# Regrouping the selection chains and moving evictions in a Fourier and mixture-of-experts kernel

## The chip, the cores and the metric

The kernel runs on one core of a Trainium2 chip. The metric is the time of one execution on the device, in microseconds (us); lower is better. A time is the median of several runs. The profile is of one further execution, with its own time. Engines are named as in the profile: PE is TensorE's matmul, PEld its weight load, DVE is VectorE, ACT is ScalarE, POOL is GpSimd and SP is SyncE, whose queue issues most of the transfers.

## The reference

For each of 8 batches of 3136 rows by 256 columns, a spectral layer runs first: a real Fourier transform along the rows, a complex 256x256 product with bias, a soft threshold of 0.01, and the inverse transform. Then comes a small routed network: each row gets a score, the 128 rows with the highest score in their batch go through a two-layer network, and the result is added to these rows.

```
X = rfft(x, axis=1)
Yr = Xr @ w_r - Xi @ w_i + b_r;  Yi = Xr @ w_i + Xi @ w_r + b_i
Y = soft_threshold(Yr) + 1j * soft_threshold(Yi)
x = irfft(Y, n=3136, axis=1)                      # the output, but for the routed rows
scores = einsum('bsd,d->bs', x, w_gate)
for b in range(8):
    top = argpartition(-scores[b], 128)[:128]
    h = maximum(x[b, top] @ w1, 0);  ye = h @ w2
    out[b, top] = x[b, top] + sigmoid(scores[b, top])[:, None] * ye
```

## The kernel before

**The stream.** The transform of length 3136 is split into 98 by 32. A loop over steps t (lines 588 to 616) writes out a software pipeline. A batch takes 13 steps of the middle stages and 16 items of the outer ones. In each step the loop issues, for the batch and item that it has reached: the first transform stage `s1` (16 steps ahead of the middle), the second stage `s2`, the product and threshold `spectral`, the first inverse stage `s2i`, and the last inverse stage `s1i` (17 steps behind). `s2i` of batch b is complete in program order at step 13b+13, and `s1i` of batch b at about 13b+29. `s1` works on batches 5 to 7 in steps 49 to 87 and is at its end there; `s2i` ends at step 104, and `s1i` at step 120.

Each item of `s1` is three matmuls into a PSUM tile `s` of 98x512, which is copied to SBUF tile `at`: items with an even number by ScalarE (line 406), items with an odd number by VectorE (line 404). Scratch tensors `As` and `Cs` in DRAM carry the data between the outer and the middle stages.

**The selection.** Scores come out of `s2i` with no further pass. `route` (lines 522 to 532) is a generator, a thread that the loop advances twice in each step. It waits until `s2i` is done with each batch of its group, runs `score` for it, then `select` for the whole group, then `place` for each batch in turn. `select` (lines 233 to 276) looks for the value of the 128th highest score bit by bit: with 2 bits per round it takes 17 rounds, with 3 bits per round 12. A round is a chain: VectorE makes candidate thresholds (`f`, line 247), compares the scores with them (`c`, line 250) and counts along rows (`n`, line 255); PE sums the counts over the partitions (`tot`, line 260); VectorE compares the totals (`ok`, `d`, lines 270 and 272) and updates the value (`w`, line 273). A group of more than one batch takes one round per step, a group of one batch two. The groups before are batches 0 to 2, batches 3 and 4 (2 bits each), and 5, 6 and 7 alone (3 bits each). The last thread, batch 7's, is issued at high priority. `place` (lines 278 to 324) turns the threshold into 128 row numbers, `idx`, one small tile for each batch.

**The routed network (FFN below).** `fetch` gathers a batch's selected rows from the output in DRAM (line 329, on POOL's queue) once its `s1i` is issued and its `idx` exists, with at most two batches fetched and not done. `ffn` takes the batches in order: four ticks of waiting, `prepare` (two transposes, line 337, and their copy to `xT`), `hidden` twice (16 matmuls each, line 354, then ScalarE makes `hh` and VectorE `hl`), `combine` (24 matmuls, line 366, then VectorE makes `ye` and POOL's queue scatters it, line 369). These two threads advance once in each step, so a batch takes eight steps. Their instructions on PE are kept behind the `s1i` matmul of the same step. Batches 0 to 3 use PSUM tile `m`, a single buffer that `score`, `select` and `place` use too; batches 4 to 7 use the tiles `px` and `py` of the middle stages. For the last batch but one, `combine` waits until the last batch is fetched, and the last batch's `prepare` is issued ahead of it. After the loop, the threads that are left are advanced until they end.

Counted in the code before: the chain of batches 0 to 2 has its rounds in steps 41 to 58, that of 3 and 4 in 67 to 84, batch 5's in 80 to 86, batch 6's in 93 to 99 and batch 7's in 106 to 112. `combine` falls in steps 67, 75, 83, 93, 101, 109 and 120 for batches 0 to 6; batch 7's FFN comes after the loop.

Of the kernel before, what the change touches and what calls it, by code (L numbers as in the profile page):

```python
# [12 lines left out]
BF16 = mybir.dt.bfloat16  # L13
U32 = mybir.dt.uint32
# [5 lines left out]
B, S, D = 8, 3136, 256  # L20
N1, N2 = 98, 32
# [87 lines left out]
def fourier_moe(ctx: ExitStack, tc: tile.TileContext, x, w_r, w_i, b_r, b_i, wg, w1, w2,  # L109
# [3 lines left out]
    NCHK = -(-cap // 128)  # L113
    const = ctx.enter_context(tc.tile_pool(name="const", bufs=1))
    pool = ctx.enter_context(tc.tile_pool(name="work", bufs=2))
# [10 lines left out]
    def c_tile(shape, dt, name):  # L126
        t = const.tile(shape, dt, name=name)
        size = int(np.prod(shape[1:])) * (2 if dt == BF16 else 4)
        placed[0] += -(-size // 32) * 32
        if placed[0] % 64:  # L130
            const.tile([128, 8], F32, name=name + "_pad")
            placed[0] += 32
        return t
# [23 lines left out]
    nrow = c_tile([N1, 1], F32, "nrow")  # L157
    tcol = c_tile([128, NCHK], F32, "tcol")
    scores = c_tile([N1, B, N2], F32, "scores")
    digits = c_tile([N1, 256], U32, "digits")  # L160

    def queued(eng, f):
# [70 lines left out]
    def select(bs, bits, thrs):  # L233
        nb = bs.stop - bs.start
        tag = f"_{bs.start}"
        sv = scores[:, bs, :].rearrange("p b (o c) -> p b o c", o=1)
        cuts = [31]
        while cuts[-1] > 0:
            cuts.append(max(cuts[-1] - bits, 0))
        w = None  # L240
        for hi, i in zip([32] + cuts, cuts):
            m = 2 ** (hi - i) - 1
            f = pool.tile([N1, nb, m], U32, name="f" + tag, bufs=1)
            if w is None:
                nc.vector.memset(f, 0)
            else:
                nc.vector.tensor_tensor(out=f, in0=digits[:, 8 * i:8 * i + m].rearrange("p (o m) -> p o m", o=1).broadcast_to([N1, nb, m]),
                                        in1=w.broadcast_to([N1, nb, m]), op=ALU.bitwise_xor)
            c = pool.tile([N1, nb, m, N2], BF16, name="c_5" if nb == 1 else "c" + tag, bufs=1)
            nc.vector.tensor_tensor(out=c, in0=sv.broadcast_to([N1, nb, m, N2]),  # L250
                                    in1=f.bitcast(F32).rearrange("p b (m o) -> p b m o", o=1).broadcast_to([N1, nb, m, N2]),
                                    op=ALU.is_ge)
            n = pool.tile([N1, nb, m], BF16, name="n" + tag, bufs=1)
            with nc.allow_low_precision(reason="counts up to 28 are exact"):
                nc.vector.tensor_reduce(out=n, in_=c, axis=AX.X, op=ALU.add)
            yield
            if nb > 1:
                yield
            tot = ps.tile([N1, nb, m], F32, name="m", bufs=1)
            nc.tensor.matmul(tot, ones, n, start=True, stop=True)  # L260
            w2 = pool.tile([N1, nb, 1], U32, name="w" + tag)
            if w is None:
                nc.vector.tensor_scalar(out=w2.bitcast(I32), in0=tot, scalar1=cap - 0.5, scalar2=1.0, op0=ALU.is_ge, op1=ALU.subtract)
            else:
                d = pool.tile([N1, nb, 1], U32, name="d" + tag, bufs=1)
                if m == 1:
                    nc.vector.tensor_scalar(out=d, in0=tot, scalar1=cap - 0.5, scalar2=None, op0=ALU.is_ge)
                else:
                    ok = pool.tile([N1, nb, m], F32, name="ok" + tag, bufs=1)
                    nc.vector.tensor_scalar(out=ok, in0=tot, scalar1=cap - 0.5, scalar2=None, op0=ALU.is_ge)  # L270
                    with nc.allow_low_precision(reason="whole numbers"):
                        nc.vector.tensor_reduce(out=d, in_=ok, axis=AX.X, op=ALU.add)
                nc.vector.scalar_tensor_tensor(out=w2, in0=d, scalar=i, in1=w, op0=ALU.logical_shift_left, op1=ALU.bitwise_xor)
            w = w2
        for b in range(bs.start, bs.stop):
            thrs[b] = w.bitcast(F32)[:, b - bs.start, :]

    def place(b, thr, slots):
        m = pool.tile([N1, 2, N2], BF16, name="mask")
        nc.vector.tensor_scalar(out=m[:, 0, :], in0=scores[:, b, :], scalar1=thr, scalar2=None, op0=ALU.is_gt)  # L280
        nc.vector.tensor_scalar(out=m[:, 1, :], in0=scores[:, b, :], scalar1=thr, scalar2=None, op0=ALU.is_equal)
        mf = m.rearrange("p a c -> p (a c)")
        yield
        pt = ps.tile([2 * N2, N1], F32, name="m", bufs=1)
        nc.tensor.matmul(pt, mf, eye, start=True, stop=True)
        mt = pool.tile([2 * N2, N1], BF16, name="mt")
        nc.vector.tensor_copy(mt, pt)
        yield
        pp = ps.tile([N1, 2, N2], F32, name="m", bufs=1)
        nc.tensor.matmul(pp.rearrange("p a c -> p (a c)"), mt, upper[:2 * N2, :], start=True, stop=True)  # L290
        row = pool.tile([N1, 2, N2 + 2], F32, name="row")
        nc.vector.tensor_copy(row[:, :, :N2], pp)
        cnt = pool.tile([N1, 2], BF16, name="cnt")
        nc.vector.tensor_copy(cnt, pp[:, :, N2 - 1])
        for a in range(2):
            nc.vector.tensor_copy(row[:, a, N2 + 1:], nrow)
        yield
        pb = ps.tile([N1, 2], F32, name="m", bufs=1)
        nc.tensor.matmul(pb, lower, cnt, start=True, stop=False)
        nc.tensor.matmul(pb[:, 1:2], ones, cnt[:, 0:1], start=False, stop=True)  # L300
        nc.vector.tensor_copy(row[:, :, N2], pb)
        end = pool.tile([N1, 2], F32, name="end")
        nc.vector.tensor_tensor(out=end, in0=row[:, :, N2], in1=row[:, :, N2 - 1], op=ALU.add)
        for k in range(NCHK):
            n = min(128, cap - 128 * k)
            hot = pool.tile([N1, 2, n], F32, name="hot", bufs=1)
            io = iota[:N1, 128 * k:128 * k + n]
            for a in range(2):
                nc.vector.tensor_scalar(out=hot[:, a, :], in0=io, scalar1=row[:, a, N2:N2 + 1], scalar2=None, op0=ALU.is_ge)
                nc.vector.scalar_tensor_tensor(out=hot[:, a, :], in0=io, scalar=end[:, a:a + 1], in1=hot[:, a, :],  # L310
                                               op0=ALU.is_lt, op1=ALU.mult)
            yield
            pi = ps.tile([n, N2 + 2], F32, name="m", bufs=1)
            for a in range(2):
                nc.tensor.matmul(pi, hot[:, a, :], row[:, a, :], start=(a == 0), stop=(a == 1))
            r = pool.tile([n, 1], F32, name="r")
            nc.vector.tensor_tensor(out=r, in0=tcol[:n, k:k + 1], in1=pi[:, N2:N2 + 1], op=ALU.subtract)
            le = pool.tile([n, N2], F32, name="le")
            c = pool.tile([n, 1], F32, name="col")
            nc.vector.tensor_scalar(out=le, in0=pi[:, :N2], scalar1=r, scalar2=None, op0=ALU.is_le)  # L320
            nc.vector.tensor_reduce(out=c, in_=le, axis=AX.X, op=ALU.add)
            idx = pool.tile([n, 1], U32, name=f"idx{b}_{k}", bufs=1)
            nc.vector.tensor_tensor(out=idx, in0=c, in1=pi[:, N2 + 1:], op=ALU.add)
            slots[b, k] = idx

# [66 lines left out]
    def s1(b, i):  # L392
        if i == 0:
            As[b] = dram.tile([N1, N2, D], F32, name="As")
        if i % 2 == 0:
            at[b] = pool.tile([N1, 4, D], F32, name="at", bufs=3)
        o = 2 * (i % 2)
        p = ps.tile([N1, 2, D], F32, name="s", bufs=4)
        if b == 0:
            nc.tensor.matmul(p, w1f, xt.pop((b, i))[:, o:o + 2, :], start=True, stop=True)  # L400
        else:
            mm3(p, w1h, w1l, *xs.pop((b, i)))
        if i % 2:
            nc.vector.tensor_copy(at[b][:, o:o + 2, :], p)
        else:
            nc.scalar.copy(out=at[b][:, o:o + 2, :], in_=p)
        if i % 2 == 1:
            (nc.gpsimd if b == 0 or b == 1 and i < 6 else nc.sync).dma_start(out=As[b][:, 2 * i - 2:2 * i + 2, :], in_=at[b])
# [155 lines left out]
            yield  # L564
            fetched.pop(0)

    threads = [route(slice(0, 3), 2), route(slice(3, 5), 2)] + [route(slice(b, b + 1), 3) for b in range(5, B)]
    ffns = [fetch(), ffn()]
    urgent = threads[-1]

# [75 lines left out]
```

## Time and profile before

| what | us |
|---|---|
| median of 3 runs (785.35 to 786.97) | 785.4 |
| the profiled execution | 784.7 |
| its span, first to last instruction | 782.9 |
| VectorE busy | 560.8 |
| ScalarE busy | 478.8 |
| GpSimd busy | 362.7 |
| mean granted PE clock | 0.978 |

The span lies within the profiled execution, which is 0.7 us below the median. A busy time is the sum of stretches in which an engine ran an instruction. PE's busy time is modelled, so that the busy time of its weight loads is read beside it. The windows view gives the same busy times for parts of the span, with the count of instructions in parentheses, and at the end the granted clock, the busy share of the DMA engines and the rate in GB/s.

### The profile page before, as it was taken

Reading aid. Unit: us, or ns where it says so; the run is one execution under the profiler, and the core shown is the slowest. Engines: PE = TensorE matmul, PEld = TensorE weight load, DVE = VectorE, ACT = ScalarE, POOL = GpSimd, SP = SyncE. Lnnn points to the kernel's source line nnn. Section 1 sums busy time; section 2 is a strip of 40 time slices with the busy share of each in tenths; the row PEclk is TensorE's granted clock in tenths of the full one; section 3 lists DMA queues with packets and bytes.
Section 4 is the critical chain, followed back from the end, with each engine's and each line's share of the span. In section 5 each row is a group of like instructions: output and inputs, shape, how many; then the busy total and the mean of one; then the engine's idle time right before and its main releaser. Section 6 shows DMA issues by size and latency. Waiting matters only on the chain. (4 is left out here: it accounts for less than half of the span.)

```text
span 782.9 us, 14996 instructions
## 1 busy us (share of the span) xinstructions
PE 729.6 (93%) x5206; PEld 644.5 (82%) x5206; DVE 560.8 (72%) x1499; ACT 478.8 (61%) x970; POOL 362.7 (46%) x382
## 2 busy tenths in 40 slices
PE   6489999999999999989999999999989999999894
PEld 2179999998999898878888898898878899887654
DVE  1347776665666679998987768888989867985651
ACT  1356667778787767667767757757644565655140
POOL 1364445556565655546455645456423332333001
PEclk9799999999999999999999999999999999999897
DMA  8798867978878877678767667657634564633740
GB/s 222 239 332 270 253 208 245 304 240 274 242 238 268 269 236 247 206 220 247 230 203 237 213 207 221 205 171 230 205 121 140 179 183 122 209 113 100 232 157 21
DMA packets 86825, 165.58 MB, mean 212 GB/s; under 512 B 6589, under 2 KB 59358, under 8 KB 86750
## 3 DMA queue, kind: packets, MB, share of 16 engines
q1 hardware_dynamic: 83070, 154.58, 62.9%
q0 software_dynamic: 3568, 10.02, 4.1%
q8 instruction: 41, 0.67, 0.4%
q14 instruction: 34, 0.28, 0.1%
q10 hardware_dynamic: 112, 0.04, 0.1%
HBM read 86.56 MB, written 78.12 MB: 210 GB/s over the span
## 5 line engine op out<-in xcount | busy, mean ns | idle before, releaser
L225 POOL TENSOR_TENSOR cl<-cv,ch 98x512 fp32r<-98x512 f32 x112 | 144.8, 1295 | 197.7 <-ACT ch L223 166.0
L225 POOL TENSOR_TENSOR xl<-xt,xh 98x512 fp32r<-98x512 f32 x112 | 144.4, 1293 | 75.9 <-ACT xh L223 69.2
L466 ACT COPY ct<-s 128x512 f32<-128x512 f32 (+1 forms) x104 | 59.3, 570 | 169.4 <-PE s L231 140.8
L229 PE MATMUL py<-wrh,Xh 128*128 128x256 f32 x400 | 120.7, 302 | 0.9 <-ACT Xh L428 0.7
L425 PEld LDWEIGHTS px<-g_sb,av 128*128 128x128 f32 (+1 forms) x800 | 104.3, 191 | 15.6 <-issue 1.9
L230 PE MATMUL py<-wrh,Xl 128*128 128x256 f32 x400 | 112.2, 280 | 0.0
L231 PE MATMUL py<-wrl,Xh 128*128 128x256 f32 x400 | 111.9, 280 | 0.0
L229 PE MATMUL py<-wih,Xh 128*128 128x256 f32 x400 | 111.9, 280 | 0.0
L231 PE MATMUL py<-wil,Xh 128*128 128x256 f32 x400 | 111.9, 280 | 0.0
L230 PE MATMUL py<-wih,Xl 128*128 128x256 f32 x400 | 111.8, 279 | 0.0
L425 PE MATMUL px<-g_sb,av 128*128 128x128 f32 (+1 forms) x800 | 108.3, 276 | 1.6 <-DMA av<-As 1.2
L470 DVE CUSTOM_DVE_ANT_0 junk<-s,wgb 128x256 f32<-128x256 f32 (+1 forms) x200 | 84.2, 421 | 28.7 <-ACT ct L466 25.8
L225 DVE TENSOR_TENSOR Yl<-py,Yh 128x512 fp32r<-128x512 f32 (+1 forms) x104 | 69.4, 667 | 38.8 <-ACT Yh L223 38.5
L445 DVE TENSOR_TENSOR py<-py,bias 128x512 f32<-128x512 f32 (+1 forms) x104 | 70.1, 674 | 34.9 <-PE py L231 34.5
L447 ACT ACTIVATE r<-py,m2l 128x512 f32<-128x512 f32 (+1 forms) x104 | 70.2, 675 | 25.5 <-DVE py L445 23.1
L430 DVE TENSOR_TENSOR Xl<-px,Xh 128x512 fp32r<-128x512 f32 (+1 forms) x104 | 69.2, 666 | 21.4 <-ACT Xh L429 17.5
L223 ACT CAST xh<-xt 98x512 fp32r<-98x512 f32 x112 | 71.3, 642 | 14.9 <-DMA xt<-in_x 10.1
L229 PEld LDWEIGHTS py<-wrh,Xh 128*128 128x128 f32 x400 | 75.7, 189 | 4.2 <-issue 2.0
L229 PEld LDWEIGHTS py<-wih,Xh 128*128 128x128 f32 x400 | 75.6, 189 | 3.0 <-issue 2.9
L230 PEld LDWEIGHTS py<-wrh,Xl 128*128 128x128 f32 x400 | 75.7, 189 | 1.5 <-issue 1.4
L231 PEld LDWEIGHTS py<-wrl,Xh 128*128 128x128 f32 x400 | 75.2, 188 | 0.9 <-issue 0.8
L231 PEld LDWEIGHTS py<-wil,Xh 128*128 128x128 f32 x400 | 75.4, 189 | 0.4 <-issue 0.3
(139 smaller groups left out, 1793.6 us busy)
## 6 DMA issues: line engine op xcount, KB each, us to landing
av<-As SPq DMA_DIRECT2D x48, 512.0 KB
Cs<-ct SPq DMA_DIRECT2D x48, 512.0 KB
xt<-in_x SPq DMA_DIRECT2D x60, 392.0 KB
out<-ot SPq DMA_DIRECT2D x60, 392.0 KB
cv<-Cs SPq DMA_DIRECT2D x59, 392.0 KB
As<-at SPq DMA_DIRECT2D x53, 392.0 KB
As<-at POOLq DMA_DIRECT2D x11, 392.0 KB, 6.6
gip<-t_gi POOLq DMA_DIRECT2D x6, 512.0 KB, 8.0
```

The source lines that it names most:

```text
L223: nc.scalar.copy(out=h, in_=src)
L225: track[sub] = sub.tensor_tensor(out=l, in0=src, in1=h.bitcast(F32), op=ALU.subtract).ins
L229: nc.tensor.matmul(out, wh, mh, start=start, stop=False)
L230: nc.tensor.matmul(out, wl, mh, start=False, stop=False)
L231: return nc.tensor.matmul(out, wh, ml, start=False, stop=stop).ins
L425: nc.tensor.matmul(px[:, 2 * p + h, :], a[:, 2 * (g % 2) * (w - 1) + p, h * 128:(h + 1) * 128], g_sb[:r, 2 * g + p, :], start=True, stop=True)
L430: nc.vector.tensor_tensor(out=xl[:, :, NF:], in0=px, in1=xh[:, :, NF:].bitcast(F32), op=ALU.subtract)
L445: nc.vector.tensor_tensor(out=py, in0=py, in1=bias[:, :w, :], op=ALU.add)
L447: nc.scalar.activation(out=r1, in_=py, func=AF.Relu, bias=m2l, scale=1.0)
L466: nc.scalar.copy(out=c, in_=p)
L470: nc.vector.tensor_tensor_reduce(out=junk[:r], in0=c[:, k, :], in1=wgb[:r], scale=1.0, scalar=0.0, op0=ALU.mult, op1=ALU.add, accum_out=Cs ...
```

## The change

It has four parts. The selection groups become batches 0 to 3, batches 4 and 5, and 6 and 7 alone. From batch 5 on, ScalarE copies every `s1` tile to SBUF, the odd ones too. The row numbers of all batches are columns of one persistent tile `idxs`, in place of eight tiles. The chains of single batches share a buffer for `c` under another name, since batch 5 no longer has a chain of its own.

```diff
     scores = c_tile([N1, B, N2], F32, "scores")
+    idxs = c_tile([128, B * NCHK], U32, "idxs")
     digits = c_tile([N1, 256], U32, "digits")
...
-            c = pool.tile([N1, nb, m, N2], BF16, name="c_5" if nb == 1 else "c" + tag, bufs=1)
+            c = pool.tile([N1, nb, m, N2], BF16, name="c_6" if nb == 1 else "c" + tag, bufs=1)
...
-            idx = pool.tile([n, 1], U32, name=f"idx{b}_{k}", bufs=1)
+            idx = idxs[:n, NCHK * b + k:NCHK * b + k + 1]
...
-        if i % 2:
+        if i % 2 and b < 5:
             nc.vector.tensor_copy(at[b][:, o:o + 2, :], p)
         else:
             nc.scalar.copy(out=at[b][:, o:o + 2, :], in_=p)
...
-    threads = [route(slice(0, 3), 2), route(slice(3, 5), 2)] + [route(slice(b, b + 1), 3) for b in range(5, B)]
+    threads = [route(slice(0, 4), 2), route(slice(4, 6), 2)] + [route(slice(b, b + 1), 3) for b in range(6, B)]
```

## The prediction

> **What bounds the kernel now.** I read the page's head first, then busy times over stretches of one batch each, then the groups of the selection chain, then the last 30 us of the timeline.
>
> ```profile
> span 782.9 us, 14996 instructions
> PE 729.6 (93%) x5206; PEld 644.5 (82%) x5206; DVE 560.8 (72%) x1499; ACT 478.8 (61%) x970; POOL 362.7 (46%) x382
> ```
>
> The profiled execution took 784.7 us, 1.8 beyond its span and 0.7 under the median of 785.4. No engine but PE is near its limit on average, and the chain that ended last explains little. So I cut the span. The first six windows hold 13 middle steps each (steps 26-39, 39-52, 52-65, 65-78, 78-91, 91-104; I call the last five S1 to S5), the seventh the last `s1i` items (S6), the eighth the tail.
>
> ```profile
> 193.70:272.30 78.60, 78.60 (x582) 71.70 (x581) 49.62 (x114) 60.81 (x126) 49.98 (x52) 1.00 0.83 254
> 272.30:358.00 85.70, 81.90 (x596) 73.67 (x595) 75.34 (x180) 59.68 (x121) 45.83 (x46) 1.00 0.73 229
> 358.00:445.40 87.40, 83.91 (x611) 75.13 (x610) 73.89 (x200) 61.35 (x123) 49.08 (x48) 1.00 0.73 230
> 445.40:540.90 95.50, 93.81 (x708) 86.18 (x708) 76.98 (x189) 62.65 (x126) 48.21 (x49) 1.00 0.64 201
> 540.90:638.30 97.40, 91.19 (x667) 81.67 (x666) 86.19 (x272) 55.81 (x115) 40.42 (x42) 0.98 0.54 168
> 638.30:721.20 82.90, 79.92 (x625) 74.75 (x624) 63.88 (x194) 47.60 (x96) 26.73 (x29) 1.00 0.43 137
> 721.20:759.20 38.00, 34.82 (x167) 22.57 (x166) 23.65 (x100) 14.54 (x30) 4.79 (x4) 0.91 0.65 205
> 759.20:782.90 23.70, 12.40 (x82) 11.50 (x80) 3.21 (x7) 1.96 (x4) 2.96 (x3) 0.78 0.14 47
> ```
>
> Columns after the length: PE, PEld, DVE, ACT, POOL. In the first row no chain and no FFN runs: PE never rests and its weight loads take 71.70/78.60 = 0.912. I take that as PE's full rate. PEld divided by 0.912 is then what PE alone would need: 80.8, 82.4, 94.5, 89.6 and 82.0 us in S1 to S5, so that 4.9, 5.0, 1.0, 7.8 and 0.9 us are **lost to something else**, 19.6 in all. They are lost where DVE is busiest (88, 85, 81, 88, 77%).
>
> What DVE does there is the chain. The same windows for line 273 alone, DVE busy and the rounds counted:
>
> ```profile
> 272.30:358.00 85.70, 9.21 (x10) 1.00 0.73 229
> 358.00:445.40 87.40, 3.77 (x6) 1.00 0.73 230
> 445.40:540.90 95.50, 7.11 (x10) 1.00 0.64 201
> 540.90:638.30 97.40, 7.98 (x17) 0.98 0.54 168
> 638.30:721.20 82.90, 3.95 (x11) 1.00 0.43 137
> ```
>
> S4 holds 17 of them, the end of one chain beside the whole chain of batch 5, and loses most.
>
> **The change, part by part: the chains.** A round's four larger operations, for three batches and for one:
>
> ```profile
> L247 DVE TENSOR_TENSOR f<-digits,w 98x9 uint32<-98x9 uint32 x15 | 7.8, 518 | 0.3
> L250 DVE TENSOR_TENSOR c<-scores,f 98x288 bf16<-98x288 f32 x15 | 10.0, 663 | 0.4
> L255 DVE TENSOR_REDUCE n<-c 98x9 bf16<-98x288 bf16 x15 | 6.7, 449 | 0.1
> L273 DVE SCALAR_TENSOR_TENSOR w<-d,w 98x3 uint32<-98x3 uint32 x16 | 13.0, 812 | 0.3
> L247 DVE TENSOR_TENSOR f<-digits,w 98x7 uint32<-98x7 uint32 x30 | 6.6, 219 | 0.8
> L250 DVE TENSOR_TENSOR c<-scores,f 98x224 bf16<-98x224 f32 x30 | 13.8, 460 | 0.7
> L255 DVE TENSOR_REDUCE n<-c 98x7 bf16<-98x224 bf16 x30 | 11.5, 385 | 0.5
> L273 DVE SCALAR_TENSOR_TENSOR w<-d,w 98x1 uint32<-98x1 uint32 x33 | 10.8, 328 | 0.7
> 320.13 1.29 POOL L225 TENSOR_TENSOR cl<-cv,ch 98x512 fp32r<-98x512 f32 x1 [2.77 <-ACT ch L223]
> 320.34 1.10 DVE L273 SCALAR_TENSOR_TENSOR w<-d,w 98x3 uint32<-98x3 uint32 x1
> ```
>
> The sums are 2.44 us (three batches) and 1.39 (one). Line 273 moves three numbers per partition in 0.81 us on average: in the last two rows it starts inside a POOL operation and ends with it (321.4). Waiting is thus a price per operation, not per batch. The fourth batch makes `c` and `n` a third longer: from the 98x224 to the 98x288 rows `n` grows by 1.0 ns for each element, so 96 more cost 0.1 us in each of the two, 0.2 to 0.4 with `f` and the waits; I take 0.3. Over 17 rounds that is 5 us of DVE added. Gone is batch 5's chain, about 12 x 1.39 = 17 us of DVE and 12 matmuls, 2 us of PE order.
>
> **Evictions.**
>
> ```profile
> L404 DVE COPY at<-s 98x512 f32<-98x512 f32 x64 | 43.8, 685 | 28.7 <-PE s L400 11.7 <-DMA As<-at 6.5 <-PE s L231 5.5
> L406 ACT COPY at<-s 98x512 f32<-98x512 f32 x64 | 38.3, 599 | 23.1 <-PE s L400 10.0 <-DMA As<-at 8.2 <-PE px L425 4.4
> ```
>
> 24 copies move: DVE loses 16.4 us, ACT gains 14.4, that is 5.5 and 4.8 for each batch, in steps 49 to 87. ACT comes to about 66 of 83 us in S2, 80%, where the first row of the windows has it at 77% with PE at full rate. I cost this at nothing; the bounds are 0 and 14.4.
>
> **Index columns and the name of `c`:** nothing. If writes to the shared tile had to wait for earlier gathers, the closest pair is two steps, some 13 us, apart. DVE runs in order, so a shared `c` adds no wait.
>
> **What moves.** Counted in the code, batches 0-3 now have rounds in steps 54-71, places in 71-80 and `combine` in steps 80, 88, 96 and 104; batches 4 and 5 have rounds in 80-97, places in 97-101, `combine` in 112 and 120. Batches 6 and 7 are routed when they were. **Batch 6's FFN falls out of the loop into the tail**, and 3's `combine` into S6. Prices for that:
>
> ```profile
> L354 PE MATMUL m<-xT,w1s 128*128 128x128 f32 x128 | 15.6, 275 | 0.0
> 324.77 0.39 PE L229 MATMUL s<-xh,w1p 98*98 98x512 f32 x1
> 325.47 1.05 PE L425 MATMUL px<-g_sb,av 128*128 128x128 f32 x8
> 757.26 1.88 PE L508 MATMUL s<-xt,w1tf 98*98 98x512 f32 x4
> 758.57 0.68 PE L229 MATMUL px<-w2h,hh 128*128 128x256 f32 x1
> 761.73 0.28 PE L231 MATMUL px<-w2l,hh 128*128 128x256 f32 x1
> 762.05 0.48 DVE L368 SCALAR_TENSOR_TENSOR ye<-px,ga,xe 128x256 f32<-128x256 f32 x1 [3.86 <-PE px L231]
> 764.15 0.98 POOL L329 DMA_INDIRECT xe<-out,idx  x1 [0.34 <-issue]
> 767.07 0.66 PE L337 MATMUL m<-ident,xe 128*128 128x128 f32 x2 [5.05 <-DMA xe<-out,idx]
> 768.25 5.88 PE L354 MATMUL py<-xT,w1s 128*128 128x128 f32 x32 [0.52 <-DVE xT L339]
> 777.98 0.99 POOL L369 DMA_INDIRECT out<-ye,idx  x1 [12.85 <-DVE ye L368]
> ```
>
> `hidden` takes 15.6/4 = 3.9 us of PE, `combine` 3.4 (758.57 to 762.01), an `s1` item 0.70 (324.77 to 325.47), so `s1` is 0.86 of each step.
>
> By stretch, each from the nearest stretch with the same mix:
> - S1 has no chain: the first row, 78.6, **-7.1**.
> - S2 has 11 rounds of four and no place: S1's mix before, with DVE's 11 x 0.3 added and 5.5 off. PE needs the free stretch's 78.6 and 1.6 for 11 chain matmuls, 80.2; I let the loss of 4.9 fall by the 2.2 that DVE gains, to about 2.5: 82.7 against 87.4, **-4.7** (-7 to 0).
> - S3 has 6 rounds of four, four places, one `prepare`: S2's mix before (87.4) with one more place (about +1 on PE) and DVE's evictions gone (about -2), some 86.5 against 95.5, **-9** (-13 to -5). Two FFNs have left it, 15 us of PE; that is why the gain is the largest here.
> - S4 has two FFNs and 11 rounds of two: S3's mix before (95.5), with three steps that have no `s1` (-2.6) and the rest of the fourth place (+1 to +2): up to 94.9, I take 95 against 97.4, **-2.4** (-5 to +2).
> - S5 has 6 rounds of two, 12 of one, three places and FFN 2: S4's mix before (97.4), ten steps without `s1` (-8.6), 3's `hidden` added (+4.3), DVE eased by six evictions (4.1 us, of which I count 2): 91.1 against 82.9, **+8.2** (+2 to +14). The low end has none of S4's 7.8 lost, the high end nearly twice as much, since rounds of two chains, three places and two FFNs meet in nine steps.
> - S6 gets 3's `combine`: at most 3.4, at least 0, since PEld is 59% busy there; **+1.5**.
> - Tail, from the last `s1i` matmul's end (759.14): `combine` of 5 as 6's before, its `px` free at 762.5 (+3.4); `prepare` and copy of 6 1.2 us (767.07 to 768.25); `hidden` 3.9 or 5.9; 7's rows are in by then or about then (+7.9); 7's `prepare` and 6's `combine` 0.7 and 3.4, and 0.3, an estimate, for the wait on `hl`; `hidden` 3.9 or 5.9; then 3.85 to the scatter as before (774.13 to 777.98). Sum 20.7 or 24.7 against 18.84 before: +1.8 or +5.8; I take **+3**.
>
> The 3.9 or 5.9 is PE's clock: the tail's window has 0.78 granted, and 32 matmuls took 5.88 us after an idle of 5.05, against 3.9 in the stream. With batch 6's work in that gap PE need not rest. The Trainium skill (TensorE: Matmul & The Clock Gate, What's actually happening) says that an idle window of about 3.4 us halves the clock and a busy one restores it; the trace agrees as far as it goes, and by the page alone the tail would be +1.8 and the sum a microsecond lower.
>
> Sum: -7.1 - 4.7 - 9 - 2.4 + 8.2 + 1.5 + 3 = **-10.5**. From 784.7 that is 774.2, and from the median 775.
>
> The gathers on POOL's queue move too. Each waits there until its batch's output has landed, with POOL's subtractions queued behind it:
>
> ```profile
> POOL xe L329 <- DMA out<-ot: 3.1, 1, 3.1
> ```
>
> Batches 5 and 6 were gathered within a step of their last `s1i`; now it is twelve and seven steps later, so this wait goes, for 0 to 3 us. POOL is idle over a third of the time there, so I take nothing. Batch 7's gather stays behind the scatter before it, as it was, and behind its own stores.
>
> **The rivals.**
> - *TensorE binds, and the losses stay.* All that helps is PE work that leaves S1 to S5: one FFN (7.8 with `prepare`), 3's `combine` (3.4), 12 chain matmuls (2), 13 in all; S6 and the tail take back 3.4 and 1.8 to 5.8: -4 to -8, near 779. For it: PEld at 86 to 90% in S1 to S4. Against it: DVE's rows. The Trainium skill (Perfetto Trace Analysis, Identifying the Most-Contended Engine) has TensorE judged by weight-load busy time; by that page PE is the contended engine and this is the outcome.
> - *Slower: batch 6's FFN stands bare in the tail.* 7's transposes are queued on PE ahead of 6's `combine`; if 7's gather comes late, PE waits, and 6's work hides nothing. A bare FFN is 13.8 us (764.15 to 777.98). With 3.4 in S6 that is +17, over the 15 that S1 to S5 give: +2, and with only the 8 to 10 of a binding PE +8: 787 to 794. It decides once the tail grows by more than S1 to S5 give.
> - *ScalarE becomes the wait.* If all 14.4 us reached PE, -10.5 becomes +4; if two thirds, no change: 784 to 787.
> - *Two chains beside each other cost nothing this time*, as `s1` is gone: S5 -8 against the forecast, 762 to 768. Against it, a wait that S5 can meet again, PE behind DVE over tile `m`:
>
> ```profile
> PE m L260 <- DVE hl L358: 4.8, 3, 2.8
> ```
>
> **How the numbers follow.** Forecast (768 to 778) 0.58, TensorE binds (778 to 783) 0.15, S5 free 0.09, ScalarE 0.05, bare tail 0.13. A measurement of this kernel tells about 0.2%, 1.6 us, from no change. Faster 0.82, same 0.05, slower 0.13. The range leaves out the bare tail and half of the lowest case: 766 to 786.
>
> **What would show it.** S1 at 78 to 79 us and DVE near 50 busy there. S2 and S3 shorter than 84 and 88. S5 the only longer stretch, with DVE over 85% and several waits on `m`. No idle gap of 5 us on PE in the tail, `hidden` near 3.9, and a span after the last `s1i` matmul 2 to 6 us longer. I am wrong if S5 exceeds 97, if PE waits on line 406 more than a few us, or if the tail grows by over 8.

## The result, and the profile after

The changed kernel takes 764.56 us (760.79 to 765.08, 4 runs) where the kernel before, run beside it, takes 786.18: a ratio of 0.9711, with a 95% interval of 0.9673 to 0.9749. Run again later beside other kernels it took 763.96, a ratio of 0.975 (0.971 to 0.979). The forecast was 775, with a range of 766 to 786: the sign was right, but the gain, forecast at 10.5 us, is 20 to 22, and 764.56 lies below the range. The profiled execution after took 764.08.

The head of the page after:

```profile
span 762.3 us, 14892 instructions
PE 726.8 (95%) x5194; PEld 645.3 (85%) x5194; DVE 520.5 (68%) x1406; ACT 489.5 (64%) x994; POOL 363.1 (48%) x382
```

VectorE has lost 40 us of work, PE and its weight loads have what they had, in a span 20.6 us shorter. The windows view after, for the same stretches of the program as in the prediction (steps 26-39, S1 to S5, S6, tail), with the columns PE, PEld, DVE, ACT, POOL, granted clock, DMA:

```profile
192.30:271.60 79.30, 79.30 (x581) 72.35 (x580) 49.81 (x114) 60.97 (x126) 49.99 (x52) 1.00 0.83 255
271.60:350.90 79.30, 79.30 (x582) 72.36 (x581) 48.52 (x112) 60.01 (x123) 45.91 (x46) 1.00 0.76 245
350.90:433.70 82.80, 82.10 (x596) 74.20 (x595) 68.37 (x172) 63.55 (x129) 46.77 (x46) 1.00 0.75 235
433.70:520.10 86.40, 84.37 (x610) 75.71 (x609) 69.52 (x194) 64.76 (x131) 48.69 (x48) 1.00 0.74 230
520.10:613.70 93.60, 93.05 (x709) 86.08 (x708) 69.91 (x196) 59.73 (x122) 40.37 (x42) 1.00 0.56 174
613.70:698.50 84.80, 80.67 (x619) 74.17 (x617) 74.65 (x262) 48.52 (x98) 27.40 (x30) 1.00 0.44 137
698.50:735.50 37.00, 34.63 (x182) 22.92 (x180) 23.19 (x89) 14.22 (x29) 5.01 (x5) 0.95 0.63 205
735.50:762.30 26.80, 19.77 (x149) 18.74 (x148) 8.27 (x25) 3.07 (x6) 3.93 (x4) 0.87 0.11 35
```

| stretch | before | after | change | forecast |
|---|---|---|---|---|
| S1 | 85.7 | 79.3 | -6.4 | -7.1 |
| S2 | 87.4 | 82.8 | -4.6 | -4.7 |
| S3 | 95.5 | 86.4 | -9.1 | -9 |
| S4 | 97.4 | 93.6 | -3.8 | -2.4 |
| S5 | 82.9 | 84.8 | +1.9 | +8.2 |
| S6 | 38.0 | 37.0 | -1.0 | +1.5 |
| tail | 23.7 | 26.8 | +3.1 | +3 |

With -0.7 from the time before S1, the column of changes gives the 20.6 us of the span. Two terms are off by more than 2 us: S5 by 6.3 and S6 by 2.5.

### The profile page after: what moved, and what is told of

It is laid out like the page before. It is cut to its first block, busy times and chain, and to the rows that moved or that the text cites. A ratio compares the mean times of both kernels' runs of the same rounds, so it can differ in the third digit from the quotient of the medians.

```text
span 762.3 us, 14892 instructions
## 1 busy us (share of the span) xinstructions
PE 726.8 (95%) x5194; PEld 645.3 (85%) x5194; DVE 520.5 (68%) x1406; ACT 489.5 (64%) x994; POOL 363.1 (48%) x382
## 4 chain that ended last, share of the span: by engine, by line
PE 79%; DVE 9%; DMA 5%; issue 3%; ACT 2%; POOL 1%; SPq 0%; POOLq 0%; ACTq 0%; DVEq 0%
PE py L230 11%; PE py L232 11%; PE py L231 11%; PE px L426 10%; PE s L232 9%; PE s L230 9%; PE s L231 9%; PE m L355 2%; DMA av<-As 1%; PE py L355 1%; PE s L401 1%; DVE w L274 1%; DMA xt<-in_x 1%; DVE c L251 1%; PE s L509 1%
## 5 line engine op out<-in xcount | busy, mean ns | idle before, releaser
L448 ACT ACTIVATE r<-py,m2l 128x512 f32<-128x512 f32 (+1 forms) x104 | 70.4, 677 | 10.5 <-DVE py L446 5.9
```

Source lines behind the costliest of these rows:

```text
L448: nc.scalar.activation(out=r1, in_=py, func=AF.Relu, bias=m2l, scale=1.0)
```

## The experiments

Two readings of the gain were to be told apart. Theory A has PE wait for a VectorE that the chains and evictions overload. The other (B, later L) has the gain come from the FFNs, which start later because the first group ends later: work leaves full stretches for S6 and the tail, where PE had time to spare. Ratios below are to the kernel before, run beside each.

**Evictions alone** (the kernel before):

```diff
-        if i % 2:
+        if i % 2 and b < 5:
```

> The kernel before with the evictions moved alone: ScalarE copies all first-stage tiles from batch 5 on. Theory A (PE waits for a VectorE that the selection chains overload): 16.4 us leave VectorE in S2 to S4, which lost 13.8 us to it, so some 4 us come off: about 782. Rival B (the gain is the FFN that falls into the idle tail): no change, 785 to 787. Rival C (ScalarE's 14.4 us more become a wait): 790 or more.

Measured: 776.2 us, 0.9894 (0.9862 to 0.9926). B and C fall, and A's 4 us were too few: it is 8, half of the 16.4 us of copies that left DVE. S4 alone went from 97.4 to 92.8 us, and DVE there from 86.19 to 79.90:

```profile
536.10:628.90 92.80, 89.33 (x668) 80.65 (x667) 79.90 (x266) 58.50 (x121) 40.06 (x41) 1.00 0.57 174
```

**The groups without the evictions** (the change with line 404's condition as before):

```diff
-        if i % 2 and b < 5:
+        if i % 2:
```

> The change without the moved evictions: groups 0-3, 4-5, 6, 7 and the index columns. A: most of the gain stays, 21.6 less some 4, about 769. B: all of it stays, 765. If the evictions are what lets the larger groups pay, over 775.

Measured: 772.45 us, 0.9838 (0.9806 to 0.987), between A and the third reading. Its S2 prices the fourth batch, since before the same 11 rounds with three batches stood in S1 (85.7 us, DVE 75.34):

```profile
354.50:442.80 88.30, 84.14 (x594) 75.35 (x593) 78.21 (x180) 59.84 (x121) 45.90 (x45) 0.98 0.71 219
```

2.6 us more, and 2.9 of DVE, where the prediction had 3.3. Not all of the 2.6 is the fourth batch's: the stretch before it, without a chain, takes 79.3 us here and 78.6 before, which the index columns below explain. With the evictions moved, S2 is 82.8: 5.5 less, as much as DVE's evictions in a batch.

**The late FFN alone** (the kernel before, its old groups):

```diff
-        if main_pe[0] is not None:
+        if main_pe[0] is not None and t >= 73:
```

> The kernel before with its groups, but the FFN threads start at step 73 as they do after the change, so that the FFN of batch 6 falls into the tail and every FFN piece sits in the step that it has after the change. B: this is where the gain comes from, 768 to 772, with the tail 3 us longer. A: only the PE work that fills an idle tail, 7.8 us less 3, is won: about 781, and the stretch of steps 78 to 91 keeps its two chains and its lost 8 us.

Measured: 770.78 us, 0.9818 (0.9784 to 0.9853). This is what B has, and A's 781 falls. S3 to S6 and the tail:

```profile
443.30:529.40 86.10, 83.75 (x605) 76.20 (x604) 75.22 (x183) 61.04 (x123) 46.09 (x46) 0.98 0.73 226
529.40:628.30 98.90, 94.34 (x714) 85.89 (x713) 82.10 (x272) 56.99 (x116) 40.76 (x43) 1.00 0.51 160
628.30:706.80 78.50, 76.61 (x604) 71.74 (x603) 64.83 (x196) 48.11 (x99) 25.56 (x28) 1.00 0.48 153
706.80:743.50 36.70, 34.29 (x182) 22.97 (x180) 23.41 (x89) 14.20 (x29) 6.10 (x6) 0.95 0.64 208
743.50:770.00 26.50, 19.77 (x148) 18.71 (x148) 8.15 (x25) 3.18 (x6) 3.93 (x4) 0.88 0.11 36
```

S3 gives 9.4 us, S5 4.4, S4 takes 1.5 back and the tail 2.8. S6 holds the `combine` of batch 3 on top and is 1.3 us shorter, not longer.

**Old groups, late FFN and moved evictions together** (the two edits above, in the kernel before):

> The kernel before with its old groups and idx tiles, the FFN threads from step 73, and the evictions on ScalarE from batch 5 on. L: the regrouping itself gains nothing, so this is as fast as the change, 761 to 766. A: the chain of batch 5 is still there beside that of 3 and 4, so some 5 us of the gain are missing, 769 or more.

Measured: 765.86 us, 0.9759 (0.9704 to 0.9813): as fast as the change, within the intervals. On its face the regrouping gains nothing beyond the delay that it causes. The stretches show that it does something, and that something else takes it back:

```profile
271.20:355.30 84.10, 82.19 (x595) 73.66 (x594) 72.41 (x178) 60.82 (x123) 46.75 (x46) 1.00 0.76 235
439.80:521.30 81.50, 80.92 (x599) 73.90 (x598) 63.38 (x175) 64.57 (x132) 44.60 (x45) 1.00 0.75 236
521.30:622.50 101.20, 96.01 (x719) 87.94 (x718) 79.71 (x266) 60.24 (x122) 42.18 (x44) 0.98 0.51 161
622.50:701.00 78.50, 76.63 (x604) 71.77 (x603) 65.04 (x196) 48.02 (x98) 25.60 (x28) 1.00 0.48 150
```

S1 and S4 are 4.8 and 7.6 us longer than after the change (the chain of three in S1, batch 5's in S4), S3 and S5 4.9 and 6.3 shorter. S1 to S5 together take 429.8 us here and 426.9 after the change.

**The index columns.** In the kernel before alone:

```diff
+    idxs = c_tile([128, B * NCHK], U32, "idxs")
...
-            idx = pool.tile([n, 1], U32, name=f"idx{b}_{k}", bufs=1)
+            idx = idxs[:n, NCHK * b + k:NCHK * b + k + 1]
```

> The kernel before with the index columns in one persistent tile alone. All theories: no change, 785 to 787.5. A wait on the shared tile would show as a VectorE wait for a gather before line 324.

Measured: 788.79 us, 1.0054 (1.0026 to 1.0082). All theories missed: it costs 4 us, with the same number of instructions on every engine. The change with the old idx tiles was run twice:

> The changed kernel with eight small idx tiles from the pool as before, in place of the columns of one persistent tile. If the 4 us that the persistent tile cost the kernel before are its own: 760 to 762. If they come of where that build's tiles happened to lie: no fixed sign, 761 to 769.

> The changed kernel with the pool's idx tiles once more, to compare it with the change on one chip: 757 to 761, 4 to 6 us under the change, with the chain-free stretch at 78.6 us on both theories.

> The changed kernel once more, beside the others on one chip: 763 to 766 on all theories.

Measured: 758.53 us, 0.9681 (0.9625 to 0.9737), and 762.35 us, 0.9709 (0.9669 to 0.975) beside 763.96, 0.975 (0.971 to 0.979), for the change. The sign agrees each time; the intervals overlap, so that this version is likely some us faster than the change and not shown to be. Two runs tell the tile from its place. An unused tile of 64 bytes in the kernel before, and a wider idxs in the change:

```diff
+    const.tile([128, 16], F32, name="shift")
```

```diff
-    idxs = c_tile([128, B * NCHK], U32, "idxs")
+    idxs = c_tile([128, 32 * NCHK], U32, "idxs")
```

> The kernel before with an unused tile of 64 bytes a partition where idxs would stand, and its eight idx tiles as they were. P: 786 to 791, 0.5% slower than before, with the chain-free stretch at 79.3 us. T: no change, 783 to 786.

> The changed kernel with idxs four times as wide, 128 bytes a partition in place of 32 and its padding to 64, so that every tile placed after it lies 128 bytes and not 64 beyond its place without idxs. Theory P (the tiles placed after idxs lie badly by 64 bytes, and PE's product with w_i reads them 3% slower): the chain-free stretch is back at 78.6 us, the total at 758 to 760. Theory T (the persistent tile itself costs: its dependences): 764 to 766 as after the change.

Measured: 788.49 us, 1.0058 (1.0033 to 1.0084), for the unused tile: nothing depends on it, so the shift of the other tiles is enough to cost this. In the chain-free stretch, by groups, first of the kernel before (193 to 272 us), then with the unused tile:

```profile
L229 PE MATMUL py<-wih,Xh 128*128 128x256 f32 x50 | 13.9, 278 | 0.0
```

```profile
L230 PE MATMUL py<-wih,Xh 128*128 128x256 f32 x50 | 14.2, 283 | 0.0
```

and with the unused tile the stretch takes 79.30 us, before 78.60:

```profile
191.70:271.00 79.30, 79.30 (x581) 72.36 (x580) 49.72 (x114) 60.88 (x127) 50.01 (x52) 1.00 0.83 256
```

After the change it is 79.30 too, with the old idx tiles 78.60. The wider idxs did not bring it back: 766.53 us, 0.9771 (0.973 to 0.9813), and 79.30 us in the stretch, though the same matmuls are nearly back at 278 ns there:

```profile
L230 PE MATMUL py<-wih,Xh 128*128 128x256 f32 x50 | 13.9, 279 | 0.0
```

So the half of theory P that names 64 bytes falls, and the 5 ns of this row do not explain the 0.7 us of the stretch; which places are slow, and why, is open.

**How late is best.** Earlier (two ticks of waiting) and later (from step 81), both in the changed kernel:

```diff
-            for _ in range(4):
+            for _ in range(2):
```

> The changed kernel with two ticks of waiting in place of four for each FFN, so that a batch's FFN takes six steps and that of batch 6 ends within the loop, at step 120; only batch 7's is in the tail. Theory L (the gain of the late FFN is that the last stretches have idle TensorE time for a whole FFN): the gain of the move is given back, 7 to 13 us, 772 to 777, with the tail 3 us shorter than after the change. Theory A (relief of VectorE from chains is the gain): no change from 764.6, within 2.

```diff
-        if main_pe[0] is not None:
+        if main_pe[0] is not None and t >= 81:
```

> The changed kernel with the FFN threads from step 81 on, eight steps later still: batch 5's FFN falls into the tail too. L with the idle time used up (TensorE is busy 19.8 of the tail's 26.8 us after the change): the loop wins 8, the tail loses 7 to 9, no change from 764.6, within 3. If the tail still had room for an FFN: 757 to 760. A: no change.

Measured: 773.93 us, 0.9843 (0.9772 to 0.9915), as L has it; and 786.86 us, 1.003 (1.0005 to 1.0054), as nothing had it. Of what the earlier start loses, 4.6 us lie in S6 (41.6 us), where PE waited 3.9 us for gathered rows, so that not all of it is PE work in full stretches. The later start, S4, S6, the tail, and the slow part of S6:

```profile
524.00:612.00 88.00, 86.54 (x652) 79.70 (x651) 68.36 (x193) 59.67 (x120) 38.17 (x41) 1.00 0.59 184
696.90:739.70 42.80, 35.59 (x107) 17.32 (x106) 18.17 (x68) 11.89 (x25) 4.02 (x4) 0.68 0.53 164
739.70:785.30 45.60, 34.88 (x282) 32.53 (x279) 16.57 (x51) 6.85 (x14) 6.86 (x7) 0.96 0.12 39
709.90:737.20 27.30, 23.47 (x45) 9.83 (x45) 12.52 (x52) 5.65 (x10) 0.00 (x0) 0.50 0.49 155
```

Against the change, S4 gave the 5.6 us of an FFN, but the tail took 18.8, and S6, with 75 matmuls fewer, became 5.8 us longer: there VectorE waited 5.5 us for gathered rows (last section). Another 4 us lie ahead of the chain-free stretch, where the two kernels do the same.

**No two chains beside each other in S5** (the change, batches 4 and 5 in chains of their own):

```diff
-    threads = [route(slice(0, 4), 2), route(slice(4, 6), 2)] + [route(slice(b, b + 1), 3) for b in range(6, B)]
+    threads = [route(slice(0, 4), 2)] + [route(slice(b, b + 1), 3) for b in range(4, B)]
```

> The changed kernel with batches 4 and 5 each in a chain of their own (3 bits, 12 rounds), so that their rounds fall in steps 67 to 73 and 80 to 86, their places end by step 76 and 89, and steps 91 to 104 keep the chain of batch 6 alone, without places of 4 and 5; every FFN stays in its step. Theory M (two chains and three places beside each other cost the stretch of steps 91 to 104 what TensorE does not need there, 84.8 - 74.17/0.912 = 3.5 us): that stretch takes 81 to 82 us, what is added earlier (24 rounds for 17) is hidden or costs up to 3, total 761 to 766. Theory N (that stretch is set by TensorE's own work and the meeting costs nothing): it stays at 84 to 85.

Measured: 779.13 us, 0.9928 (0.989 to 0.9966). M holds for S5: 79.4 us is 5.4 less, and just what PE needs (72.45/0.912 = 79.4). The 3.5 us are gone, as M has it, and the other 1.9 are PE's own work, whose need was 81.3. Theory N falls. The total missed: S3, where batch 4's rounds now meet the first chain, is 16.4 us longer, and S4 5.3. S3 and S5:

```profile
436.00:538.80 102.80, 93.89 (x630) 83.02 (x629) 87.98 (x279) 65.46 (x132) 48.95 (x48) 0.93 0.63 193
637.70:717.10 79.40, 77.67 (x605) 72.45 (x604) 64.73 (x196) 47.96 (x98) 25.52 (x28) 1.00 0.48 150
```

The same kind of meeting is thus dearer in S3, where `s1` and its POOL subtractions run (POOL 48.95 us busy), than in S5, where they have ended (27.40 after the change); that POOL is the reason is not shown. S3 also has 20 more matmuls than after the change, one more chain of 12 rounds and a granted clock of 0.93, so that the 16.4 are not the meeting's alone.

## Why the prediction was right and where it was wrong

The step that failed is the term of S5, forecast at +8.2 us and measured at +1.9, and after it that of S6, +1.5 for -1.0. Together they are 8.8 of the 10.1 us by which the sum fell short of the gain in the spans.

**Right: what is lost, and to what.** In S1 to S4 the forecast by stretch is within 1.5 us. S1 without a chain runs as the chain-free stretch does, 79.30 and 79.30. The fourth batch cost 2.9 us of DVE for 3.3; of the DVE time that the evictions freed, half was gained. Of the 19.6 us that PE had lost some 8 are left: by the same sum the lost time after is 0, 1.4, 3.4, 0 and 3.5 us. This is some 12 of the 22 us by which S1 to S5 became shorter; the other 10 are PE's own need, 429.3 us before and 419.4 after. That DVE was where the time went is borne out by the run with the evictions alone.

**Right: ScalarE.** ACT is at 63.55 of 82.8 us in S2, 77% for the 80% forecast, and the evictions alone gained 8 us.

**Right: the tail.** It grew by 3.1 us for 3 forecast. PE's rows of the tail, after:

```profile
734.49 1.02 PE L509 MATMUL s<-xt,w1tf 98*98 98x512 f32 x2
740.63 0.44 PE L338 MATMUL px<-ident,xe 128*128 128x128 f32 x2 [0.83 <-DVE ye L369]
741.58 5.46 PE L355 MATMUL py<-xT,w1s 128*128 128x128 f32 x32 [0.52 <-DVE idxs L324]
746.88 0.38 PE L338 MATMUL m<-ident,xe 128*128 128x128 f32 x2
749.93 3.74 PE L355 MATMUL py<-xT,w1s 128*128 128x128 f32 x32
```

Batch 6's `prepare` starts 5.1 us after the last `s1i` matmul (forecast 3.4): 5's `combine` shares PE with batch 7's `place`. Batch 7's transposes (746.88) find their rows there, and with 6's `combine` they take 3.05 us, to 749.93, where the forecast had 4.4, 0.3 of it a wait on `hl` that no row shows. Its `hidden` takes 3.74 us at full clock, not 5.88. Batch 6's still took 5.46: the granted clock was halved for 3.4 us from 741.6. The sum was right, in part by luck: the late `prepare` and the short `combine` cancel, and one `hidden` of two ran in part at half clock.

**Wrong: S5, "S4's mix before (97.4), ten steps without `s1` (-8.6), 3's `hidden` added (+4.3), DVE eased by six evictions (-2)".** The steps counted were right, but S4's mix was the wrong one to start from, and two sizes were off. First, PE's own work: the mix makes PE's need fall by 4.3 us, and measured by weight loads over 0.912 it fell from 89.6 to 74.17/0.912 = 81.3, by 8.3. S4 before contains work of the next batch, which PE has begun ahead of the window's edge; S5 is the last stretch and has no next batch. The windows view of `s2` alone (tile g_sb; PE, PEld), in S4 before:

```profile
540.90:638.30 97.40, 14.12 (x100) 13.11 (x100) 0.98 0.54 168
```

and in S5 after:

```profile
613.70:698.50 84.80, 10.96 (x78) 10.11 (x76) 1.00 0.44 137
```

The same for the product (tile Xh; PE, PEld, DVE, ACT), in S4 before:

```profile
540.90:638.30 97.40, 40.40 (x200) 31.98 (x200) 8.61 (x13) 11.60 (x26) 0.98 0.54 168
```

and in S5 after:

```profile
613.70:698.50 84.80, 37.08 (x184) 29.37 (x184) 7.22 (x11) 9.97 (x22) 1.00 0.44 137
```

S5 before has the same count as S5 after:

```profile
638.30:721.20 82.90, 36.37 (x184) 29.24 (x184) 7.23 (x11) 9.85 (x22) 1.00 0.43 137
```

It also has the 64 matmuls of `hidden` that S5 after has, two FFNs in both. So the nearest neighbour was S5 itself: the prediction has its need at 82.0 us, after it is 81.3, and only the second chain and the places of 4 and 5 were left to price.

The two tiles differ by 6.5 us of busy PE between S4 before and S5 after, which the mix left in, partly offset by an `s1` that was priced too high: 33 of its matmuls touch S4's window before, and ten steps were priced at 37. Second, the loss: 7.8 us in S4 before, taken as 5.8 in S5, was 3.5. Two rows of the kernel before show a part of it that did not recur. A matmul of the timeline, with the idle time before it:

```profile
580.01 0.17 PE L260 MATMUL m<-n,tm 98*98 98x6 bf16 x1 [2.76 <-DVE hl L358]
```

and the windows view right behind it:

```profile
581.40:584.90 3.50, 3.50 (x16) 3.18 (x15) 2.41 (x11) 0.93 (x2) 0.00 (x0) 0.51 0.00 0
```

PE rested 2.76 us for tile `m`, and then ran 3.5 us at a granted clock of 0.51. S5 after has a granted clock of 1.00 throughout. The two sizes make 4.0 and 2.3 of the 6.3 us.

**Wrong: S6, "+1.5".** Forecast between 0 and 3.4, it came out at -1.0. Batch 7's chain runs through most of this stretch, and 3's `combine` fitted in beside it; the granted clock rose from 0.91 to 0.95, and the late FFN alone gave the same (36.70 us). In the run without the evictions the stretch took 35.9 us with as many matmuls (182) and a clock of 1.00, so that much of the 1.0 can lie in how long the clock is halved. That work in the gaps of a chain is free in general is not shown.

**Wrong: index columns, "nothing".** There is no wait, as argued, but the tile's place costs 0.7 us in a stretch of 79, some 4 us in all. It took back about what the regrouping gained: without the tile the changed kernel is 4 to 7 us faster than old groups with late FFN and evictions (758.53 and 762.35 against 765.86), with intervals that overlap. The stretches say the same: S1 to S5 take 425.0 us without the tile (758.53 us run), against 429.8 with the old groups.

**The rivals.** "TensorE binds" had the FFN's part right and gave back 3.4 us in S6 that were never asked for. The bare tail did not come with the change; it came with the later start, and decided there as forecast: the tail grew by more than the loop gave. "Two chains cost nothing" was nearest in total, and wrong in its reason: S5 lost 3.5 us, and nothing in the run without the meeting.

So the gain of 20 us is made up of about 14 from the later FFN, 8 from the evictions, which together give 19 and not 22, some 5 from the regrouping itself (an estimate from the runs above, whose intervals overlap), and 4 lost to the place of a tile.

## What to carry to other kernels

When a stretch is priced by another that has the same mix, count the instructions of both windows first: an engine that runs ahead carries the next stretch's work into one and not into the other; the same stretch of the kernel before comes first. Before a regrouping is credited, delay alone should be tried, since work that comes later may gain by where it lands: a `combine` cost nothing visible beside a chain in S6, an FFN 3 us in a half-idle tail, and the next one 19 us in the same tail. And a change of declarations alone can move a kernel by 0.5%, which is as much as many edits are worth.

## What the runs showed of the hardware

**A late gather held up a chain, and half clock followed.** With the later start (step 81) S6 took 42.8 us with 107 matmuls (granted clock 0.68), after the change 37.0 with 182 (0.95). The missing PE work is not what shows as the cause. A gather issued at 703.07 us took some 8 us to land. VectorE waited for its rows at line 343 of `prepare`, and the chain's count `n` was behind that in VectorE's order, so that PE waited too:

```profile
711.42 0.43 DVE L343 CUSTOM_DVE_ANT_0 junk<-xe,wgb 128x256 f32<-128x256 f32 x1 [5.50 <-DMA xe<-out,idxs]
712.21 0.17 PE L261 MATMUL m<-n,tm 98*98 98x7 bf16 x1 [5.34 <-DVE n L256]
```

In all PE waited 6.6 us for `n` in this stretch, against 2.0 after the change, which is 4.6 of the 5.8 us. The clock was halved from 709.9 to 737.2 us, and stayed so although the records have PE busy without a gap from 713 to 728 us (weight loads 5.09 of these 15 us). What the half clock alone cost is not shown. The Trainium skill (TensorE: Matmul & The Clock Gate, What's actually happening) has the clock halve after an idle window of about 3.4 us; the half-clock stretches here last 3.4 us or multiples of it (3.4 from 741.6 after the change, 27.3 here), which agrees with the length of the window. The idle gaps ahead of two of them were shorter, 2.76 us in S4 before, and 0.83 and 0.52 us after the change, so that these traces do not show a whole window of idle to be needed; no run here varied the gap.

**The place of a tile changes the speed of PE.** 64 bytes more ahead of the work tiles make the chain-free, PE-bound stretch 0.9% longer: 79.3 to 79.9 us in eight profiles of kernels with the shift, 78.6 to 78.7 in six without. With these 64 bytes the matmuls of one product take 283 ns in place of 278. 128 bytes brought these back to 279 ns and left the stretch at 79.3 us.
